# Ten instead of eight weight pairs of the second half's second layer as seven products

## The chip, the cores and the metric

The kernel runs on one core of one Trainium2 chip, with float32 in and out. The time is the device time of the program in microseconds (us); of several executions the median is given. The core has a matrix engine (TensorE, "PE" in the profile, its weight loads "PEld"), VectorE (DVE), ScalarE (ACT), GpSimd (POOL) and SyncE (SP), which here only issues DMAs. Each engine runs its own instructions in the order in which they stand in the program, and an instruction whose data is late holds up everything behind it on that engine.

## The reference

One block on 2048 tokens of width 576: `out = x + attention(layernorm(x)) @ wo + mlp(layernorm(x))`.

```python
xn = layernorm(x)                              # [1, 2048, 576]
q, k, v = heads(xn @ wqkv)                     # 32 heads of 18
idx = pos[:, None] - 2 * arange(8)             # window of 8, dilation 2
attn = softmax(where(idx >= 0, einsum("bhsd,bhswd->bhsw", q, k[idx]) * 18**-0.5, -1e9))
a = einsum("bhsw,bhswd->bhsd", attn, v[idx]).reshape(1, 2048, 576) @ wo
h = einsum("bsd,df->bsf", xn, w1) + b1         # F = 4608
m = einsum("bsf,fd->bsd", h * tanh(softplus(h)), w2)
return x + a + m
```

## The kernel before, in words

**Halves.** The tokens are worked in two halves of 1024 (`hf` 0 and 1). In each half come the projections to query, key and value (`qkv_item`, and `z_part` in the second half), and then the MLP, with the attention of the same half woven in between. At the end `wo_part` multiplies the attention's output by `wo`.

**Numbers in two parts.** Every matrix operand is kept as a rounded high part and a low part, the remainder: a "high" step is a cast on ScalarE, a "low" step a subtraction on VectorE or GpSimd. A product of two such operands takes three matmuls.

**The MLP by pairs.** F is cut into 36 blocks of 128, and two blocks make a pair `q`, 0 to 17. `m1_part` makes the hidden activations of a pair in parts 0 to 5. The second layer of a pair is multiplied one pair later. In the first half, and in the second half from some pair on, that is four chunks of 24 matmuls each (`m2_pair`, line 780; `m2_cols`, line 893). The earlier pairs of the second half go another way: two pairs together (index `e`) are taken as a 2x2 block product by seven products in place of eight (`p_item`, line 872). One such product, an item `k` of 0 to 6 named in `ORD`, is 24 matmuls as a chunk is. `OC` is the number of such twos; with `OC = 4` these are pairs 0 to 7, and pair 8 (`2 * OC`) goes by chunks again, with its activations held as the earlier ones were and split by `a_split`.

**What the seven products need.** Sums of weights T1 to T4: they are made in the first half, where the weights are loaded anyway (`t_sum`, `t_high`, `t_low`, line 301 and on), written to DRAM (`t_keep`) and fetched for their item by `p_fetch`. Sums of activations S1 to S4: `u_sum` (line 814), in place, on VectorE but for two of eight. The high and low part of each left operand: `u_high` (line 820, ScalarE) and `u_low` (line 826, eight of fourteen on GpSimd). Raw activations stand in fixed buffers (`raw_act`). The item's results are added from PSUM into `accP` on VectorE (line 878, and line 876 on ScalarE for the first two); at the end `p_join` joins them.

**The order of the program.** `plan` is a list of steps. A step holds its own functions (`plan[i][0]`: a part of `m1_part`, an item, a chunk) and a list of other work (`plan[i][1]`, filled by `before(i, ...)`), which is issued ahead of them. In the second half an even pair has four items among its steps, an odd pair three:

```python
seq = (0, 1, "N", 2, "N", 3, "N", 4, "N", 5)   # even pair; "N" is an item
for i, p_ in enumerate((0, 1, 2, "N", 3, "N", 4, "N", 5))  # odd pair
```

The number of a step inside its pair is `i` in `spot(hf, q, i)`. An item is issued one `e` after its activations were made: those of pairs 0 and 1 in pairs 2 and 3, and so on.

**Attention.** It is a generator of 73 steps for a half; eight rounds (two units of two heads each) of nine steps: four products of query and key (GpSimd, line 539), one step of softmax, four products with the values (GpSimd, line 577). What VectorE does with a GpSimd product, a reduction (lines 544 and 583), is issued at the next attention step. With the softmax go lines 558 and 560 on VectorE, the exponential on ScalarE (line 564, with a table load before it and another behind it), and then lines 568 to 570. When a round is over, `oT` is transposed on VectorE (line 603). `early` says at which steps of each pair of the second half an attention step is taken; pairs that aren't in it have five.

**Waits between the engines in the second half.** The `out` tag has four PSUM banks, one for each of an item's four results; the next item needs them free again, which the additions of line 878 do. Part 4 of `m1_part` adds into the bank that VectorE reads for the activation of block (1,1) (line 725, the name `rt`), so part 4 waits for that read. These two places, the banks behind `accP` and part 4 behind `rt`, are where TensorE meets VectorE.

## Time and profile before

| | |
|---|---|
| time, median of 3 runs | 1108.59 us (1108.43 to 1108.93) |
| the profiled execution's own time | 1109.51 us |
| its span (first to last instruction) | 1107.7 us |
| granted TensorE clock | 0.999 |
| PE busy | 1100.8 us, 99% |
| VectorE busy | 850.6 us, 77% |
| GpSimd busy | 791.1 us, 71% |
| ScalarE busy | 499.1 us, 45% |
| DMA moved | 271.60 MB, mean 245 GB/s |

Matmuls are pipelined and their ends are modelled, so that a busy PE isn't proof that it runs at its peak; idle time of the other engines costs nothing by itself. Pair q of the first half begins at 24.1 us steps (pair 2 at 139.18, pair 10 at 332.12). In the second half pair 2 begins at 649.46, pair 8 at 786.45, and the last chunks end at 1050 us.

### The profile page before, as it was taken

To read this page: it belongs to the slowest core of one execution; us is meant where nothing else is said; L and a number is where in the kernel's file an instruction comes from. 1 tells how busy PE (TensorE), PEld (TensorE's weight loads), DVE (VectorE), ACT (ScalarE), POOL (GpSimd) and SP (SyncE) were. 2 spreads that over 40 slices of the span, in tenths; PEclk is the share of its full clock that TensorE was granted. 3 is DMA by queue.
4 is the path that set the end of the run, shared out by engine and by line. 5 is a ranking of instruction groups with operands and counts; after the bars stand their busy time and mean duration, and the time that the engine had idled before them with its cause. 6 is when DMAs were issued, how large, how long until landed. Compare 5 with 4: busy or idle time off the path is not lost.

```text
span 1107.7 us, 18208 instructions
## 1 busy us (share of the span) xinstructions
PE 1100.8 (99%) x6550; PEld 1015.3 (92%) x6550; DVE 850.6 (77%) x1367; ACT 499.1 (45%) x917; POOL 791.1 (71%) x639
## 2 busy tenths in 40 slices
PE   9999999999999999999999999999999999999998
PEld 8999899999999999999999888989999999999998
DVE  6368788888889888898656567777876677777786
ACT  5544655544544544545333354434433344343353
POOL 2479777776779688685789667567698976867542
PEclk9999999999999999999999999999999999999999
DMA  6899696868777768676598799656674657776674
GB/s 203 284 311 308 235 343 232 282 239 266 254 259 249 266 222 296 238 263 214 170 323 268 237 358 317 223 192 208 221 222 173 210 195 224 243 288 218 179 234 140
DMA packets 178270, 271.60 MB, mean 245 GB/s; under 512 B 53218, under 2 KB 120068, under 8 KB 178180
## 3 DMA queue, kind: packets, MB, share of 16 engines
q1 hardware_dynamic: 178180, 270.44, 72.0%
q8 instruction: 52, 0.85, 0.3%
q14 instruction: 38, 0.31, 0.1%
HBM read 160.39 MB, written 110.00 MB: 244 GB/s over the span
## 4 chain that ended last, share of the span: by engine, by line
PE 94%; DMA 2%; DVE 2%; ACT 1%; POOL 1%; issue 0%; SPq 0%; DVEq 0%; POOLq 0%
PE h L680 29%; PE po L780 21%; PE po L893 11%; PE pq L348 11%; PE po L872 6%; PE h L686 6%; PE o L1076 5%; PE z L446 4%; DMA t<-kept_t 1%; DMA accP<-in_x 1%; POOL act L732 0%; PE ta L75 0%; DMA acc<-in_x 0%; DVE st L112 0%; DVE u L826 0%
## 5 line engine op out<-in xcount | busy, mean ns | idle before, releaser
L780 PEld LDWEIGHTS po<-w,act 128*128 128x128 f32 x1728 | 236.4, 188 | 6.0 <-POOL act L732 0.4
L780 PE MATMUL po<-w,act 128*128 128x288 f32 x1728 | 240.7, 295 | 0.1
L539 POOL TENSOR_TENSOR pr<-q,kv 128x576 f32<-128x576 f32 x128 | 198.2, 1574 | 9.3 <-DMA q<-q_d 6.1
L732 POOL TENSOR_TENSOR act<-c,act 128x512 fp32r<-128x512 f32 x81 | 107.4, 1326 | 128.1 <-ACT act L731 127.3
L577 POOL TENSOR_TENSOR pv<-L,kv 128x576 f32<-128x576 f32 x128 | 178.1, 1485 | 26.3 <-DVE L L570 21.4
L784 DVE TENSOR_TENSOR acc<-po,acc 128x288 f32<-128x288 f32 x288 | 119.3, 449 | 29.7 <-PE po L780 28.9
L348 PE MATMUL pq<-wq,xt 128*128 128x432 f32 x672 | 136.3, 361 | 0.9 <-ACT xt L81 0.6
L893 PEld LDWEIGHTS po<-w,act 128*128 128x128 f32 x960 | 130.9, 188 | 2.9
L893 PE MATMUL po<-w,act 128*128 128x288 f32 x960 | 132.9, 294 | 0.0
L348 PEld LDWEIGHTS pq<-wq,xt 128*128 128x128 f32 x672 | 125.1, 188 | 7.7 <-ACT xt L81 1.3
L726 ACT ACTIVATE c<-c,b1c 128x512 f32<-128x512 f32 x81 | 58.7, 725 | 138.1 <-DVE c L725 137.8
L680 PE MATMUL h<-xt,t 128*128 128x512 f32 x432 | 110.7, 391 | 0.1
L680 PE MATMUL h<-S,t 128*128 128x512 f32 x432 | 110.5, 391 | 0.0
L583 DVE TENSOR_REDUCE og<-pv 128x144 f32<-128x1152 f32 x64 | 85.9, 1345 | 24.1 <-POOL pv L577 23.9
L680 PE MATMUL h<-xt,wa 128*128 128x512 f32 x432 | 104.1, 390 | 0.0
L714 ACT COPY c<-h 128x512 f32<-128x512 f32 x81 | 47.4, 586 | 124.1 <-PE h L686 73.1
L544 DVE TENSOR_REDUCE L<-pr 128x64 f32<-128x1152 f32 x64 | 85.8, 1342 | 20.9 <-POOL pr L539 20.8
L680 PEld LDWEIGHTS h<-xt,wa 128*128 128x128 f32 x432 | 80.9, 188 | 17.0
L872 PEld LDWEIGHTS po<-pw,u 128*128 128x128 f32 x672 | 92.1, 188 | 3.5 <-DVE accP L878 1.2
L872 PE MATMUL po<-pw,u 128*128 128x288 f32 x672 | 93.8, 295 | 0.8 <-DVE accP L878 0.8
L680 PEld LDWEIGHTS h<-xt,t 128*128 128x128 f32 x432 | 79.1, 188 | 15.1 <-DVE rt L725 0.5
L896 DVE TENSOR_TENSOR accP<-po,accP 128x288 f32<-128x288 f32 x160 | 69.0, 452 | 30.2 <-PE po L893 29.4
(228 smaller groups left out, 1854.3 us busy)
## 6 DMA issues: line engine op xcount, KB each, us to landing
kv<-kv_d SPq DMA_DIRECT2D x64, 396.0 KB, 5.2
kept_t<-t SPq DMA_DIRECT2D x36, 512.0 KB, 4.4
t<-kept_t SPq DMA_DIRECT2D x36, 512.0 KB, 6.5
rw<-in_w SPq DMA_DIRECT2D x36, 320.0 KB, 4.5
kept_wa<-wa SPq DMA_DIRECT2D x18, 640.0 KB, 4.9
kept_w<-w SPq DMA_DIRECT2D x20, 576.0 KB, 4.1
wa<-kept_wa SPq DMA_DIRECT2D x18, 640.0 KB, 5.2
w<-kept_w SPq DMA_DIRECT2D x20, 576.0 KB, 4.3
```

What stands on the lines that cost most here:

```text
L348: nc.tensor.matmul(pq[:, 0:432], XT[:, xi, tok], wt[wi][:, hl, 0:432], start=i == 0, stop=i == len(seq) - 1)
L539: nc.gpsimd.tensor_tensor(out=pr[:, x:x + hh], in0=q[:, j0 + x:j0 + x + hh, None, :].to_broadcast([P, hh, W, CU]), in1=win(kt, 0, CU, j0 + ...
L544: nc.vector.tensor_reduce(L[:, k, j0:j0 + hj].rearrange("p j w h -> p (j w h)"), pr.rearrange("p j w (h d) -> p (j w h) d", h=2), axis=AX, ...
L577: nc.gpsimd.tensor_tensor(out=pr[:, x:x + hj].rearrange("p j d w -> p j w d"), in0=L[:, k, x:x + hj, :, h:h + 1].to_broadcast([P, hj, W, DH]),
L583: nc.vector.tensor_reduce(og[:, c0:c0 + DH, :].rearrange("p d j -> p j d"), pr, axis=AX, op=ALU.add)
L680: nc.tensor.matmul(ph, wt[:, wl, wk * P:(wk + 1) * P], X[:, xs, :], start=first and i == 0, stop=last and i == len(seq) - 1, skip_group_ch ...
L732: nc.gpsimd.tensor_tensor(out=a[:, 1, :], in0=t, in1=a[:, 0, :].bitcast(F32), op=ALU.subtract)
L780: nc.tensor.matmul(po, acts[hf, q, b, j][:, al, tok], done["w2", hf, 2 * q + j][:, wl, c * HC:(c + 1) * HC], start=i == 0, stop=i == 5)
L784: nc.vector.tensor_tensor(out=t, in0=po, in1=t, op=ALU.add)
L872: nc.tensor.matmul(po, units[e, k, qq][:, al, tok], w[:, qq, wl, :], start=i == 0, stop=i == 5)
L893: nc.tensor.matmul(po, acts[hf, q, b, j][:, al, tok], done["w2", hf, 2 * q + j][:, wl, c * HC:(c + 1) * HC], start=i == 0, stop=i == 5)
L896: nc.vector.tensor_tensor(out=t, in0=po, in1=t, op=ALU.add)
```

## The change

`OC` goes from 4 to 5: pairs 8 and 9 of the second half's second layer are taken by seven products as well, and pair 10 takes the part that pair 8 had. With it go these moves:

- In the first half, T1 to T4 are made and written out for pairs 9 and 10 of the weights, too. The similar sums for the projections (`z_load` and on) begin twelve steps later and stand closer together.
- `early` is written anew: odd pairs 3, 5, 7 and 9 have four attention steps (at 0, 2, 4 and 6), even pairs 2 to 8 three (at 0, 4 and 7), and pairs 10 and 11, which had five, have the three that pairs 8 and 9 had. By the end of pair 11 the same number of steps is done as before.
- One sum of activations, S4 of the second pair for item 6 of the first two (`e = 0`, `qq = 1`), is issued behind the step's own instructions instead of ahead of them.
- The preparation of `wo` begins later (from pair 13 instead of 11), and closer together.
- One raw activation of pair `2 * OC` has another buffer than the rotation gives.

```diff
-OC = 4
+OC = 5
...
-                  (0, 1): (("raw", 3), ("mn", 4), ("mn", 1)), (1, 1): (("tt", 0), ("tt", 1))}[b, j][q % {(1, 0): 4, (1, 1): 2}.get((b, j), 3)]
+                  (0, 1): (("raw", 3), ("mn", 4), ("mn", 1)), (1, 1): (("tt", 0), ("tt", 1))}[b, j][3 if (q, b, j) == (2 * OC, 1, 0) else q % {(1, 0): 4, (1, 1): 2}.get((b, j), 3)]
...
-    i = spot(0, 9, 4)
+    i = spot(0, 10, 6)
...
-                d = 30 + 2 * n + (n >= 14) if k else 2 * n if n < 10 else (19, 20, 22, 23, 25, 26, 27)[n - 10]
+                d = 28 * k + (2 * n if n < 10 else (19, 20, 22, 23, 25, 26, 27)[n - 10])
...
-            before(s2, lambda e=e, k=k, qq=qq: u_sum(e, k, qq))
+            plan[s2][0 if (e, k, qq) == (0, 6, 1) else 1].append(lambda e=e, k=k, qq=qq: u_sum(e, k, qq))
...
-    early = {0: (8,), 1: (0, 2, 4, 6, 8), 2: (0, 4, 7), 3: (0, 3, 6), 4: (0, 4, 7), 5: (0, 3, 7), 6: (1, 4, 7),
-             7: (0, 4, 7), 8: (1, 4, 8), 9: (1, 3, 7)}
+    early = {0: (8,), 1: (0, 2, 4, 6, 8), 2: (0, 4, 7), 3: (0, 2, 4, 6), 4: (0, 4, 7), 5: (0, 2, 4, 6), 6: (0, 4, 7),
+             7: (0, 2, 4, 6), 8: (0, 4, 7), 9: (0, 2, 4, 6), 10: (1, 4, 8), 11: (1, 3, 7)}
...
-    i = spot(1, *(11,3))
+    i = spot(1, 13, 0)
...
-        k = i + 10 + (2, 5, 10, 15, 20, 25, 30, 35, 40)[n]
+        k = i + 10 + (2, 5, 8, 12, 15, 19, 23, 27, 31)[n]
```

The change moves instructions on every engine. Three places are shown, in the order of the two programs. In the names `po_0_4_1_0` is PSUM of `e` 0, item 4, second half of its tokens; `u_0_6_1` is the left operand of `e` 0, item 6, second pair; `pr_1_1_0_1` and `pv_1_1_0_1` are attention products of the second half, round 1; `h3_1_3` is a bank of pair 3.

VectorE in pair 3, around item 4 of the first two, before (line 814 is the moved sum, line 878 the additions that free the banks, the last row the read that part 4 waits for):

```order
L725 TENSOR_TENSOR ra0_7255<-h2_1_3_7761,ra0_7255 128x512
L826 TENSOR_TENSOR u_0_5_1_7793<-rm3_7262,u_0_5_1_7793 128x512
L814 TENSOR_TENSOR rm4_7263<-rm4_7263,rm3_7262 128x512
L878 TENSOR_TENSOR accP2_0_7472<-po_0_4_0_0_7811,accP2_0_7472 128x288
L878 TENSOR_TENSOR accP2_0_7472<-po_0_4_0_1_7819,accP2_0_7472 128x288
L878 TENSOR_TENSOR accP2_1_7473<-po_0_4_1_0_7827,accP2_1_7473 128x288
L878 TENSOR_TENSOR accP2_1_7473<-po_0_4_1_1_7835,accP2_1_7473 128x288
L544 TENSOR_REDUCE L_1_1_7745<-pr_1_1_0_0_7747 128x64
L826 TENSOR_TENSOR u_0_6_1_7846<-rm4_7263,u_0_6_1_7846 128x512
L725 TENSOR_TENSOR rt1_7265<-h3_1_3_7777,rt1_7265 128x512
```

The same place now:

```order
L725 TENSOR_TENSOR ra0_7289<-h2_1_3_7795,ra0_7289 128x512
L544 TENSOR_REDUCE L_1_1_7779<-pr_1_1_0_0_7781 128x64
L826 TENSOR_TENSOR u_0_5_1_7827<-rm3_7296,u_0_5_1_7827 128x512
L878 TENSOR_TENSOR accP2_0_7506<-po_0_4_0_0_7845,accP2_0_7506 128x288
L878 TENSOR_TENSOR accP2_0_7506<-po_0_4_0_1_7853,accP2_0_7506 128x288
L878 TENSOR_TENSOR accP2_1_7507<-po_0_4_1_0_7861,accP2_1_7507 128x288
L878 TENSOR_TENSOR accP2_1_7507<-po_0_4_1_1_7869,accP2_1_7507 128x288
L814 TENSOR_TENSOR rm4_7297<-rm4_7297,rm3_7296 128x512
L544 TENSOR_REDUCE L_1_1_7779<-pr_1_1_0_1_7830 128x64
L826 TENSOR_TENSOR u_0_6_1_7880<-rm4_7297,u_0_6_1_7880 128x512
L725 TENSOR_TENSOR rt1_7299<-h3_1_3_7811,rt1_7299 128x512
```

The sum stands behind the four additions; the reduction that stood there has gone ahead of the low step of item 5, and the next one, of `pr_1_1_0_1`, has come to its place.

VectorE in pair 5, the same place of the second two, before:

```order
L826 TENSOR_TENSOR u_1_5_1_8264<-ra_r_7801,u_1_5_1_8264 128x512
L814 TENSOR_TENSOR ra3_7258<-ra3_7258,ra_r_7801 128x512
L583 TENSOR_REDUCE og_1_1_8154<-pv_1_1_0_1_8222 128x8x18
L878 TENSOR_TENSOR accP2_0_7472<-po_1_4_0_0_8280,accP2_0_7472 128x288
L878 TENSOR_TENSOR accP2_0_7472<-po_1_4_0_1_8288,accP2_0_7472 128x288
L878 TENSOR_TENSOR accP2_1_7473<-po_1_4_1_0_8296,accP2_1_7473 128x288
L878 TENSOR_TENSOR accP2_1_7473<-po_1_4_1_1_8304,accP2_1_7473 128x288
L826 TENSOR_TENSOR u_1_6_1_8314<-ra3_7258,u_1_6_1_8314 128x512
L814 TENSOR_TENSOR rm2_7261<-ra1_7256,rm2_7261 128x512
L725 TENSOR_TENSOR rt1_7265<-h3_1_5_8252,rt1_7265 128x512
```

And now:

```order
L583 TENSOR_REDUCE og_1_1_8101<-pv_1_1_1_0_8264 128x8x18
L826 TENSOR_TENSOR u_1_5_1_8302<-ra_r_7841,u_1_5_1_8302 128x512
L814 TENSOR_TENSOR ra3_7292<-ra3_7292,ra_r_7841 128x512
L878 TENSOR_TENSOR accP2_0_7506<-po_1_4_0_0_8318,accP2_0_7506 128x288
L878 TENSOR_TENSOR accP2_0_7506<-po_1_4_0_1_8326,accP2_0_7506 128x288
L878 TENSOR_TENSOR accP2_1_7507<-po_1_4_1_0_8334,accP2_1_7507 128x288
L878 TENSOR_TENSOR accP2_1_7507<-po_1_4_1_1_8342,accP2_1_7507 128x288
L583 TENSOR_REDUCE og_1_1_8101<-pv_1_1_1_1_8305 128x8x18
L603 STREAM_TRANSPOSE oT_1_1_8372<-og_1_1_8101 128x576
L826 TENSOR_TENSOR u_1_6_1_8352<-ra3_7292,u_1_6_1_8352 128x512
L814 TENSOR_TENSOR rm2_7295<-ra1_7290,rm2_7295 128x512
L725 TENSOR_TENSOR rt1_7299<-h3_1_5_8290,rt1_7299 128x512
```

Ahead of the additions one reduction is gone to before the low step; between the additions and the read for part 4 there are a reduction and the transposition more.

ScalarE at the head of pair 4, where the second two begin, before:

```order
L714 COPY ra1_7256<-h1_1_4_7971 128x512
L820 CAST u_1_0_1_7990<-ra_r_7801 128x512
L726 ACTIVATE ra1_7256<-ra1_7256,b1c_122 128x512
L820 CAST u_1_1_1_8006<-rt1_7265 128x512
L820 CAST u_1_2_0_8042<-ra2_7257 128x512
```

And now:

```order
L714 COPY ra1_7290<-h1_1_4_8009 128x512
L564 ACT_TABLE_LOAD
L564 ACTIVATE L_1_1_7779<-L_1_1_7779 128x256
L820 CAST u_1_0_1_8029<-ra_r_7841 128x512
L726 ACT_TABLE_LOAD
L726 ACTIVATE ra1_7290<-ra1_7290,b1c_122 128x512
L820 CAST u_1_1_1_8045<-rt1_7299 128x512
L820 CAST u_1_2_0_8081<-ra2_7291 128x512
```

The exponential of round 1 with its two table loads now stands around the cast that item 0 needs.

More of the change, by code (lines that the diff above doesn't have):

```diff
@@ L1495, in block_kernel @@
     behind_adds.update((at["p", "x", OC - 1, 4], at["p", "x", 0, 4], at["s", 1, 2 * OC, 1]))
-    behind_next.add(at["m", 1, 10, 3])
+    behind_next.add(at["m", 1, 2 * OC + 2, 3])
     T = [0.0]
@@ L1504, in block_kernel @@
             ok[spot(0, q, i)] = i in (0, 3, 7, 9) and (q > 1 or i)
-    marks = [at["q", 0, 2, 0, 1], at["q", 0, 3, 0, 0], spot(0, 1, 0), spot(0, 2 * OC + 1, 0), at["q", 1, 0, 0, 0],
+    marks = [at["q", 0, 2, 0, 1], at["q", 0, 3, 0, 0], spot(0, 1, 0), spot(0, 9, 0), at["q", 1, 0, 0, 0],
              at["z", 0, 0], spot(1, 0, 0)]
```

## The prediction

> **What bounds the kernel now.** The page's busy times come first: TensorE is busy 99% of the span, and the next engine 77%.
>
> ```profile
> span 1107.7 us, 18208 instructions
> PE 1100.8 (99%) x6550; PEld 1015.3 (92%) x6550; DVE 850.6 (77%) x1367; ACT 499.1 (45%) x917; POOL 791.1 (71%) x639
> ```
>
> A busy PE can hide matmuls that are stretched or late, so the chain of work that ended last comes next. In the plain part (chunks of line 893) it is TensorE alone, pair after pair:
>
> ```profile
> 868.62 2.73 PE h L680 x12
> 873.16 3.18 PE po L893 x24
> ...
> 916.88 2.73 PE h L680 x12
> ```
>
> Two pairs take 916.88 - 868.62 = 48.26 us there, and 24 matmuls of the second layer 3.18 us. The busy times by stage show the part with seven products, one row for each of pairs 3, 4 and 5 (the columns: PE, PEld, DVE, ACT, POOL):
>
> ```profile
> 673.84:696.23 22.39, 21.49 (x124) 18.89 (x122) 19.08 (x25) 9.01 (x17) 18.49 (x13) 1.00 0.79 263
> 696.23:720.40 24.17, 24.17 (x147) 22.13 (x146) 18.12 (x34) 11.84 (x18) 13.79 (x11) 1.00 0.64 230
> 720.40:741.37 20.97, 20.97 (x123) 18.95 (x122) 16.06 (x25) 7.93 (x13) 14.31 (x11) 1.00 0.54 187
> ```
>
> Pairs 4 and 5 take 45.14 us together, which is 48.26 less 24 matmuls: TensorE waits for nothing there. Pair 3 takes 22.39 where pair 5, with the same matmuls, takes 20.97: 1.42 us are lost. So a change is worth what it takes from TensorE's instructions, less the waits it makes, and room is scarce in the odd pairs: VectorE is busy for 85% of pair 3 and 77% of pair 5.
>
> **The change part by part.** *The product that goes.* By the order, lines 872 and 893 have 672 and 960 matmuls before, 840 and 768 now: 24 fewer. At 3.18 us for 24 that is -3.2 us; by the two stages above, 45.14 - 48.26 = -3.1, which I take. All of it is on the path, since TensorE is the path.
>
> *The moved sum, pair 3.* VectorE alone, and then TensorE, at that place:
>
> ```profile
> 682.26 1.36 DVE L826 TENSOR_TENSOR u<-rm,u 128x512 fp32r<-128x512 f32 x1 [1.82 <-ACT u L820]
> 683.55 1.77 DVE L814 TENSOR_TENSOR rm<-rm,rm 128x512 f32<-128x512 f32 x1
> 685.24 1.54 DVE L878 TENSOR_TENSOR accP<-po,accP 128x288 f32<-128x288 f32 x4
> 686.70 1.34 DVE L544 TENSOR_REDUCE L<-pr 128x64 f32<-128x1152 f32 x1
> 687.96 0.68 DVE L826 TENSOR_TENSOR u<-rm,u 128x512 fp32r<-128x512 f32 x1
> 688.56 0.68 DVE L725 TENSOR_TENSOR rt<-h,rt 128x512 f32<-128x512 f32 x1
> ```
>
> ```profile
> 684.32 0.61 PE L686 MATMUL h<-xt,wc 128*128 128x512 f32 x2
> 685.74 3.47 PE L872 MATMUL po<-pw,u 128*128 128x288 f32 x24 [0.81 <-DVE accP L878]
> 689.29 1.43 PE L680 MATMUL h<-xt,t 128*128 128x512 f32 x5
> ```
>
> Item 5 (685.74) waits 0.81 us for the additions at 685.24, which stand behind the sum of 1.77. Without it ahead of them the additions start at 683.55, and item 5 at 684.93: that wait is gone. What is late next is part 4 (689.29), which needs the read `rt` of line 725; it could start at 684.93 + 3.18 = 688.1. The reduction that went ahead of the low step at 682.26 costs nothing: VectorE had 1.82 us idle there. Counting from start to start, the path to the read is now: additions 683.55 to 685.01 (1.46), the sum 0.6 to 1.7, a reduction 1.26, a low step 0.60, the read 0.68: 689.2 with the long sum, 688.2 with the short. The reduction moreover waits for GpSimd's `pr_1_1_0_1`:
>
> ```profile
> 676.47 2.82 POOL L539 TENSOR_TENSOR pr<-q,kv 128x576 f32<-128x576 f32 x2
> ```
>
> ```profile
> 684.73 7.04 POOL L539 TENSOR_TENSOR pr<-q,kv 128x576 f32<-128x576 f32 x4
> ```
>
> Such a product has two halves, 2.8 us in the first row and 3.5 in the second. It now starts ahead of GpSimd's own sum, at about 683.0, and ends at 685.9 to 686.6. So part 4 starts at 688.4 to 689.3, or at 690.3 if the low step too is stretched by as much as the sum. Against 689.29: -0.9 to +1.0. I take 0: the sum was long at this very place, and GpSimd is as busy there as before. So 0.81 is won at item 5 and lost again at part 4.
>
> *Four attention steps in an odd pair.* The same place in pair 5:
>
> ```profile
> 727.69 1.77 DVE L814 TENSOR_TENSOR ra<-ra,ra_r 128x512 f32<-128x512 f32 x1
> 729.38 1.34 DVE L583 TENSOR_REDUCE og<-pv 128x144 f32<-128x1152 f32 x1
> 730.65 1.53 DVE L878 TENSOR_TENSOR accP<-po,accP 128x288 f32<-128x288 f32 x4
> 732.11 0.68 DVE L826 TENSOR_TENSOR u<-ra,u 128x512 fp32r<-128x512 f32 x1
> 732.70 0.68 DVE L814 TENSOR_TENSOR rm<-ra,rm 128x512 f32<-128x512 f32 x1
> 733.31 0.68 DVE L725 TENSOR_TENSOR rt<-h,rt 128x512 f32<-128x512 f32 x1
> ```
>
> ```profile
> 734.55 1.55 PE L680 MATMUL h<-xt,t 128*128 128x512 f32 x6
> ```
>
> ```profile
> L603 DVE STREAM_TRANSPOSE oT<-og 128x576 f32<-128x576 f32 x16 | 12.4, 774 | 0.3
> L826 DVE TENSOR_TENSOR u<-rm,u 128x512 fp32r<-128x512 f32 x12 | 12.3, 1023 | 6.2 <-ACT u L820 6.2
> L814 DVE TENSOR_TENSOR rm<-ra,rm 128x512 f32<-128x512 f32 x6 | 6.9, 1152 | 0.9 <-ACT rm L726 0.9
> ```
>
> Now the additions follow the sum at 729.38, to 730.84; then a reduction (1.26), the transposition (0.77), the low step and the next sum (0.60 each), the read (0.68): 734.75 where part 4 starts at 734.55 today. That is +0.2 if nothing is stretched. In this window GpSimd was idle before and now has the fourth step's product; by the group means (1.02 for the low step and 1.15 for the sum, where 0.68 is the least) it is +1.0, and if both are stretched to 1.77, +2.4. I take +0.5. In pair 7 the same path loses the softmax's two instructions and gains one sum, and had no room left: -0.2 to +1.9, taken at +0.1. Pair 9, with lines 568 to 570 in that place, is alike: +0.1.
>
> *The exponential at pair 4.* The cast of item 0's second operand now stands behind it, and the low step behind that:
>
> ```profile
> L560 DVE TENSOR_TENSOR L<-L,m 128x256 f32<-128x256 f32 x16 | 11.7, 731 | 0.5
> ```
>
> ```profile
> L558 DVE TENSOR_REDUCE m<-L 128x32 f32<-128x256 f32 x16 | 6.7, 420 | 0.5
> ```
>
> ```profile
> L820 ACT CAST u<-ra 128x512 fp32r<-128x512 f32 x22 | 13.4, 621 | 9.9 <-DVE ra L814 5.1 <-POOL ra L814 2.6 <-PE po L872 2.1
> ```
>
> ```profile
> L564 ACT ACTIVATE L<-L 128x256 f32<-128x256 f32 x16 | 6.7, 418 | 17.3 <-DVE L L560 17.2
> ```
>
> ```profile
> 698.93 0.69 DVE L826 TENSOR_TENSOR u<-ra_r,u 128x512 fp32r<-128x512 f32 x1 [1.37 <-ACT u L820]
> ```
>
> ```profile
> 700.76 3.33 PE L872 MATMUL po<-pw,u 128*128 128x288 f32 x24
> ```
>
> VectorE's work before that low step ended at 698.93 - 1.37 = 697.56. With lines 558 and 560 (0.42 and 0.73), the exponential (0.42), the cast (0.62) and the low step (0.69) behind one another it is 700.4. The item starts at 700.76 and uses the operand's low part in its sixth matmul, 0.66 later. Cost 0, and 0.5 if the low step too is stretched.
>
> *The first half.* Pairs 9 and 10 get the sums T1 to T4. The fuller of the two before, and one of VectorE's three new instructions:
>
> ```profile
> 332.12:356.20 24.08, 24.08 (x148) 22.09 (x147) 22.16 (x32) 11.32 (x20) 22.09 (x18) 1.00 0.75 250
> ```
>
> ```profile
> L312 DVE TENSOR_TENSOR twT<-twT,twhT 128x576 fp32r<-128x576 f32 x16 | 13.8, 893 | 0.3
> ```
>
> Three of them are 2.7 us, and VectorE loses one of about that kind, the subtraction for the projections that is placed later: 22.16 + 1.8 = 24.0 of 24.08. That is full, yet TensorE's pair shows no loss at 22.2, and what runs over falls into pair 11. I take 0; counted without what goes, 24.9, it runs over by 0.8, the upper bound. The DMAs that go with them (four more writes in each of the two pairs, and later the fetches of seven more items in place of two pairs' weights) stand on SP, behind which no row shown has TensorE waiting. The later `wo` work, the other buffer and the additional splits of pairs 8 and 9 have GpSimd's and VectorE's idle time of pairs 8 to 17 as cover: 0.
>
> *Sum.* -3.1 + 0 + 0.5 + 0.1 + 0.1 = -2.4 us. The profiled execution took 1109.51 us, 0.9 over the median of 1108.59, in equal work; so it would be 1107.1 profiled, and **1106.2** as a median.
>
> **A rule weighed.** In the trace a sum of line 814 takes 0.68 us at 732.70, with GpSimd idle, and 1.77 at 683.55, beside a GpSimd instruction; the additions of line 878, which read PSUM, take the same 1.5 for four in both places. The Trainium skill, "SBUF — State Buffer", section "Who interferes with whom", says that a VectorE instruction with two SBUF inputs and a GpSimd instruction that reads SBUF block each other for the whole instruction, and that reductions never contend. By that rule every low step and sum of the path that meets a GpSimd instruction waits it out, and the time would be that of the slower rival below; by the rows alone it is -2.4. The trace agrees in part: the low step at 687.96 took 0.68 in the middle of GpSimd's products, so that there it was GpSimd that waited.
>
> **The rivals.** *The gain is eaten (no change).* All stretchable instructions of the path take their group means: pair 3 +0.4, pair 5 +1.0, pairs 7 and 9 +0.6 each, 2.6 us in all: -0.5, 1108.1. For it speaks that GpSimd was idle on this path in pairs 5 and 7 and isn't any more; against it, that in pair 5 the additions come 1.3 us earlier, since the reduction went ahead of them.
>
> *The path to part 4 becomes the bound (slower).* Low step and sum are both stretched to 1.77 in each odd pair: +1.0, +2.4, +1.9, +1.9, 7.2 in all, so +4.1, 1112.7. It decides against the change from 1.3 us for each odd pair on, and is slower by over 0.2% from 5.3 in all. Against it: in pair 3, before, one of the two was long and the other was not.
>
> *The first half runs over.* VectorE full in pair 10 delays the freeing of banks by the 0.8 us above, with the forecast's other terms: 1107.0.
>
> **How the numbers follow.** Forecast 0.50, eaten gain 0.28, first half 0.05, slower 0.17. About 0.2%, 2.2 us, is what a measurement of this kernel can tell from no change; the forecast lies just past it, the second and the third within. Faster 0.50, same 0.33, slower 0.17. The range goes from 1104.8 (pair 3 at -0.9, pair 5 at +0.2, pairs 7 and 9 at 0: -3.8; what lies below is left out with some 0.04) up to 1110.8, where slower by over 0.2% begins; most of the slower rival (0.14) is left out.
>
> **What would show it.** In the profile after: 1608 matmuls in lines 872 and 893; pairs 8 and 9 at 45.1 us together; no wait of TensorE on line 878 at item 5 of pair 3; part 4 of pair 5 waiting 0.2 to 1 us on `rt`, that of pairs 7 and 9 hardly. Wrong it would be if a pair of the first half is over 24.2 us, or if the odd pairs take over 22 us: then the waits are the larger term.

## The result, and the profile after

The changed kernel takes 1122.02 us (median of 5, 1119.87 to 1124.9) where the kernel before takes 1108.59. The medians alone give 1.0121 times as long; the ratio on record is 1.0108, with a 95% interval of 1.0082 to 1.0133. The forecast was 1106.2. The profiled execution took 1119.87 us with a span of 1118.1, 10.4 us over the span before. (Beside runs 13, 14 and 17 below, the kernel before itself took 1113.8 to 1116.1 us in half of its executions or more, so the ratios on record there, 0.9960, 1.0005 and 0.9967, mix two levels of that kernel, and these runs' times are set against its 1108.59.)

The page's busy times after:

```profile
span 1118.1 us, 18215 instructions
PE 1101.4 (99%) x6526; PEld 1013.1 (91%) x6526; DVE 861.8 (77%) x1381; ACT 503.2 (45%) x927; POOL 802.7 (72%) x647
```

The 24 matmuls are gone, but TensorE isn't busy for less time, and the span is longer. The waits of TensorE after, without those of the first microseconds (what waits, for what; us in all, how often, the longest). Of these lines the kernel before had none, only one wait of 0.8 us on line 878:

```profile
PE h L680 <- DVE rt L725: 4.3, 3, 1.5
PE h L680 <- DVE c L725: 3.0, 2, 2.3
PE po L872 <- DVE u L826: 1.6, 2, 0.8
PE po L780 <- DVE acc L784: 0.9, 2, 0.8
PE po L893 <- DVE accP L896: 0.7, 1, 0.7
```

Busy times by stage, one row for each pair that lost time: pairs 9, 11 and 15 of the first half, then 3, 5, 7 and, for comparison, 9 of the second (the columns as in the prediction):

```profile
307.51:335.86 28.35, 26.02 (x148) 23.28 (x146) 24.49 (x39) 12.58 (x21) 23.41 (x20) 0.94 0.75 263
359.94:385.12 25.18, 24.41 (x148) 22.03 (x146) 20.44 (x30) 11.65 (x18) 17.27 (x14) 1.00 0.86 316
457.43:483.00 25.57, 24.73 (x147) 22.08 (x146) 19.82 (x31) 12.48 (x22) 21.89 (x23) 1.00 0.68 248
...
680.21:702.90 22.69, 21.20 (x124) 18.94 (x122) 20.57 (x25) 8.91 (x17) 19.54 (x14) 1.00 0.78 260
727.20:751.02 23.82, 21.48 (x124) 18.97 (x122) 20.28 (x28) 7.71 (x13) 17.88 (x13) 1.00 0.62 208
775.19:798.74 23.55, 21.49 (x124) 18.97 (x122) 19.91 (x25) 7.80 (x14) 19.07 (x14) 1.00 0.58 209
822.91:843.81 20.90, 20.90 (x124) 18.91 (x122) 18.64 (x30) 10.91 (x16) 13.83 (x11) 1.00 0.62 214
```

Where the 10.4 us went, by the starts of the pairs before and after:

| place | forecast | before | after | difference |
|---|---|---|---|---|
| first half, pairs 9 and 10 | 0 | 48.23 | 52.43 | +4.2 |
| first half, pair 11 | 0 | 24.15 | 25.18 | +1.0 |
| first half, pair 15 | 0 | 24.17 | 25.57 | +1.4 |
| second half, pairs 3 and 4 | 0 | 46.56 | 46.99 | +0.4 |
| pair 5 | +0.5 | 20.97 | 23.82 | +2.85 |
| pair 7 | +0.1 | 20.90 | 23.55 | +2.65 |
| pairs 8 to 11 (the product) | -3.0 (-3.1 and +0.1) | 106.10 | 103.11 | -3.0 |
| pair 17 to the end | 0 | 94.46 | 95.56 | +1.1 |

The rest, -0.3, lies before pair 0. So the gain came as forecast, and waits that were costed at next to nothing took it back more than four times over. The places are those of one profiled execution: in other profiles of the same first half (runs 2, 5, 7 and 10) pair 9 loses 2.6 or 4.2, pair 10 between 0 and 3.6 and pair 11 between 0 and 2.0 us, 4.7 to 6.2 together. What makes pair 11's share wasn't found.

**Pair 5, after.** GpSimd, VectorE and TensorE on the path to part 4 and item 6 (the last bracket of a row is the idle time before it and what ended it):

```profile
738.48 3.31 POOL L539 TENSOR_TENSOR pr<-q,kv 128x576 f32<-128x576 f32 x2
739.74 0.76 DVE L826 TENSOR_TENSOR u<-ra,u 128x512 fp32r<-128x512 f32 x1
740.42 1.92 DVE L814 TENSOR_TENSOR rm<-ra,rm 128x512 f32<-128x512 f32 x1
742.26 0.68 DVE L725 TENSOR_TENSOR rt<-h,rt 128x512 f32<-128x512 f32 x1
742.99 1.66 PE L680 MATMUL h<-xt,t 128*128 128x512 f32 x6 [1.53 <-DVE rt L725]
744.28 1.28 POOL L826 TENSOR_TENSOR u<-rm,u 128x512 fp32r<-128x512 f32 x1 [2.49 <-ACT u L820]
744.32 1.79 DVE L826 TENSOR_TENSOR u<-rm,u 128x512 fp32r<-128x512 f32 x1
746.17 2.11 PE L872 MATMUL po<-pw,u 128*128 128x288 f32 x14 [0.81 <-DVE u L826]
```

The sum at 740.42 takes 1.92 us beside GpSimd's product, where it took 0.68 before; part 4 waits 1.53. Late from there, item 6's low step (744.32) meets a GpSimd low step, takes 1.79, and item 6 waits 0.81 more in its middle.

**Pair 9 of the first half, after.** GpSimd, ScalarE, VectorE and TensorE around the sums of weights:

```profile
320.39 0.82 POOL L301 TENSOR_TENSOR twT<-rw,twT 128x288 f32<-128x288 f32 x1
321.16 3.34 POOL L577 TENSOR_TENSOR pv<-L,kv 128x576 f32<-128x576 f32 x2
324.32 0.84 POOL L301 TENSOR_TENSOR twT<-rw,twT 128x288 f32<-128x288 f32 x1
325.19 0.67 ACT L307 CAST twhT<-twT 128x576 fp32r<-128x576 f32 x1 [4.17 <-POOL twT L301]
325.89 0.76 DVE L312 TENSOR_TENSOR twT<-twT,twhT 128x576 fp32r<-128x576 f32 x1 [2.59 <-ACT twhT L307]
326.57 0.68 DVE L725 TENSOR_TENSOR c<-h,c 128x512 f32<-128x512 f32 x1
327.31 1.92 PE L680 MATMUL h<-xt,t 128*128 128x512 f32 x4 [2.33 <-DVE c L725]
```

An attention product stands on GpSimd between the second and the third sum of weights. So the third is late, then its cast, then its low part on VectorE, and behind that the read of line 725 that TensorE needs. VectorE had been idle 2.59 us: it wasn't full, it stood behind a late operand. Before, with the same attention steps but no sums of weights in this pair, TensorE had no wait there:

```profile
307.81:331.96 24.15, 24.15 (x147) 22.11 (x146) 21.18 (x34) 10.91 (x19) 19.31 (x17) 1.00 0.74 250
```

**Pair 15 of the first half, after.** The sums of weights for the projections, which the change begins twelve steps later:

```profile
473.63 1.11 POOL L394 TENSOR_TENSOR zB<-zB,zB 128x432 f32<-128x432 f32 x1
474.77 0.61 DVE L402 TENSOR_TENSOR zB<-zB,zhT 128x432 fp32r<-128x432 f32 x1 [3.50 <-POOL zB L394]
475.29 0.68 DVE L725 TENSOR_TENSOR c<-h,c 128x512 f32<-128x512 f32 x1
476.03 1.66 PE L680 MATMUL h<-xt,t 128*128 128x512 f32 x6 [0.67 <-DVE c L725]
```

It is the same chain once more. GpSimd makes the sum T4 (line 394) late; the low step of T2 (line 402) writes over what T4 reads and stands behind it, and behind that stands the read that TensorE needs.

### The profile page after: what moved, and what is told of

Read it like the earlier page. It is cut to its first block, busy times and chain, and to the rows that moved or that the text cites. A ratio compares the mean times of both kernels' runs of the same rounds, so it can differ in the third digit from the quotient of the medians.

```text
span 1118.1 us, 18215 instructions
## 1 busy us (share of the span) xinstructions
PE 1101.4 (99%) x6526; PEld 1013.1 (91%) x6526; DVE 861.8 (77%) x1381; ACT 503.2 (45%) x927; POOL 802.7 (72%) x647
## 4 chain that ended last, share of the span: by engine, by line
PE 77%; POOL 10%; issue 5%; DVE 5%; DMA 2%; ACT 1%; SPq 0%; POOLq 0%; DVEq 0%
PE h L680 23%; PE po L780 16%; PE pq L348 11%; PE po L893 7%; PE po L872 6%; PE o L1076 5%; PE h L686 4%; PE z L446 4%; POOL pv L577 2%; POOL pr L539 2%; POOL act L732 2%; DVE u L826 1%; POOL u L826 1%; POOL tt L240 1%; DMA accP<-in_x 1%
## 5 line engine op out<-in xcount | busy, mean ns | idle before, releaser
L780 PEld LDWEIGHTS po<-w,act 128*128 128x128 f32 x1728 | 236.6, 188 | 7.6 <-DVE acc L784 1.8
L780 PE MATMUL po<-w,act 128*128 128x288 f32 x1728 | 241.0, 295 | 1.1 <-DVE acc L784 0.9
L577 POOL TENSOR_TENSOR pv<-L,kv 128x576 f32<-128x576 f32 x128 | 181.7, 1511 | 23.7 <-DVE L L570 13.7
L732 POOL TENSOR_TENSOR act<-c,act 128x512 fp32r<-128x512 f32 x75 | 99.7, 1329 | 121.2 <-ACT act L731 118.6
L872 PEld LDWEIGHTS po<-pw,u 128*128 128x128 f32 x840 | 115.3, 188 | 5.3 <-DVE u L826 2.2
L872 PE MATMUL po<-pw,u 128*128 128x288 f32 x840 | 117.8, 295 | 1.6 <-DVE u L826 1.6
L726 ACT ACTIVATE c<-c,b1c 128x512 f32<-128x512 f32 x75 | 54.4, 725 | 133.2 <-DVE c L725 133.0
L893 PEld LDWEIGHTS po<-w,act 128*128 128x128 f32 x768 | 104.6, 188 | 3.3 <-DVE accP L896 1.2
L893 PE MATMUL po<-w,act 128*128 128x288 f32 x768 | 106.3, 295 | 0.7 <-DVE accP L896 0.7
L680 PEld LDWEIGHTS h<-S,t 128*128 128x128 f32 x432 | 77.9, 188 | 13.2 <-ACT rm L714 0.5
L714 ACT COPY c<-h 128x512 f32<-128x512 f32 x75 | 43.9, 585 | 96.8 <-PE h L686 52.8
```

The costliest lines, as they stand in the source:

```text
L577: nc.gpsimd.tensor_tensor(out=pr[:, x:x + hj].rearrange("p j d w -> p j w d"), in0=L[:, k, x:x + hj, :, h:h + 1].to_broadcast([P, hj, W, DH]),
L680: nc.tensor.matmul(ph, wt[:, wl, wk * P:(wk + 1) * P], X[:, xs, :], start=first and i == 0, stop=last and i == len(seq) - 1, skip_group_ch ...
L732: nc.gpsimd.tensor_tensor(out=a[:, 1, :], in0=t, in1=a[:, 0, :].bitcast(F32), op=ALU.subtract)
L780: nc.tensor.matmul(po, acts[hf, q, b, j][:, al, tok], done["w2", hf, 2 * q + j][:, wl, c * HC:(c + 1) * HC], start=i == 0, stop=i == 5)
L872: nc.tensor.matmul(po, units[e, k, qq][:, al, tok], w[:, qq, wl, :], start=i == 0, stop=i == 5)
L893: nc.tensor.matmul(po, acts[hf, q, b, j][:, al, tok], done["w2", hf, 2 * q + j][:, wl, c * HC:(c + 1) * HC], start=i == 0, stop=i == 5)
```

## The experiments

**One part each: attention in the first half (1), three steps (2), four steps in the kernel before (3), the moved sums of the projections in the kernel before (4).**

```diff
 # 1, on the changed kernel
-spot(0, 1, 0), spot(0, 9, 0)
+spot(0, 1, 0), spot(0, 2 * OC + 1, 0)
-rate = (1.15, 0.4, 0.5, 0.8, 1.15, 1.25, 0)
+rate = (1.15, 0.4, 0.5, 0.886, 1.15, 1.25, 0)
 # 2, on the changed kernel (behind_next is emptied with it)
-3: (0, 2, 4, 6), 5: (0, 2, 4, 6), 7: (0, 2, 4, 6), 9: (0, 2, 4, 6)
+3: (0, 3, 6), 5: (0, 3, 7), 6: (1, 4, 7), 7: (0, 4, 7), 9: (0, 4, 7), 12 to 15: (0, 2, 4, 5, 7, 9)
 # 3, on the kernel before
-3: (0, 3, 6), 5: (0, 3, 7), 7: (0, 4, 7)
+3, 5, 7: (0, 2, 4, 6), 10: (1, 4, 8), 11: (1, 3, 6, 9)
 # 4, on the kernel before: the two edits to the chain of z_load and on
```

Expected of 1: 

> The changed kernel, but in the first half attention runs at its slower rate (0.5) up to pair 10, as far as sums of weights are made, and at 0.886 in place of 0.8 behind it, so that as many steps fit. If pair 9 was lost because GpSimd had attention steps at the faster rate and the sums T1 to T4 in one pair, pair 9 goes back from 28.35 to 24.15 us, 4.2 us less in all (about 1117.8 for 1122.0). If the sums alone are too much for the pair, whatever the attention does, pair 9 stays above 27 us. Pairs 11 and 15, which get a little more attention, keep their 1.0 and 1.4 us or lose up to 1 us more.

Expected of 2: 

> The changed kernel with three attention steps in place of four in pairs 3, 5, 7 and 9 of the second half (where they stood before), and six in place of five in pairs 12 to 15, where no seven-product items are left. If the fourth step makes the waits, pairs 5 and 7 go back from 23.82 and 23.55 us to 20.9 to 21.3, so that 5.0 to 5.7 us go (about 1116.5); the sixth step in the later pairs may take up to 2 of them back. If the waits come from the tenth pair's other traffic (more fetches, the moved sum, the splits), pairs 5 and 7 stay above 23 us.

Expected of 3: 

> The kernel before with nothing changed but four attention steps in pairs 3, 5 and 7 of the second half at steps 0, 2, 4 and 6, three in pair 10 and four in pair 11. If the fourth step alone makes the waits, pair 5 takes 23.8 and pair 7 23.5 us, and pair 3 about as much as before or up to 1 us more: 5.5 to 6.5 us slower than before (1114 to 1115). If it needs something else of the change beside it, pairs 5 and 7 stay under 21.5 us and the time within 1 us of 1108.6.

Expected of 4: 

> The kernel before with nothing changed but the place of the projections' weight sums: twelve steps later and closer together. If the move alone makes the waits of pairs 11 and 15 of the first half, those take 25.2 and 25.6 us and the time is 2.4 us over before (about 1111.0). If these waits come from what the sums T1 to T4 of pairs 9 and 10 push ahead of them, pairs 11 and 15 stay at 24.15 us and the time at 1108.6.

Measured: 1 takes 1119.87 us (1116.78 to 1124.34), pair 9 24.69 for 28.35; but pair 13 takes 25.12, pair 15 25.25 and the stretch from pair 17 0.7 more. 2 takes 1122.44: pairs 3, 5 and 7 take 21.51, 20.90 and 21.49 for 22.69, 23.82 and 23.55, and pairs 12 to 14 with the sixth step lose 2.9, 0.7 and 3.7. 3 takes 1116.0, ratio 1.0063 (1.0046 to 1.0079). Its pairs 5 and 7, and TensorE's wait in pair 8 for a fetch of a sum of weights, which no theory had:

```profile
721.00:744.82 23.82, 21.47 (x124) 18.97 (x123) 20.09 (x27) 7.73 (x13) 17.97 (x13) 1.00 0.63 209
...
768.99:790.93 21.94, 21.28 (x123) 19.02 (x122) 18.23 (x25) 7.92 (x14) 18.71 (x14) 1.00 0.55 182
...
PE po L872 <- DMA pw<-kept_T: 1.2, 1, 1.2
```

4 takes 1110.04, ratio 1.0015 (1.0004 to 1.0025): pair 15 takes 25.61, while pairs 9 to 11 are unhurt.

```profile
355.82:379.97 24.15, 24.15 (x147) 22.11 (x146) 22.22 (x33) 12.45 (x19) 17.53 (x14) 1.00 0.71 253
...
452.29:477.90 25.61, 24.71 (x148) 22.07 (x146) 19.81 (x31) 12.51 (x22) 21.92 (x23) 1.00 0.67 248
```

What follows: the fourth step alone makes the whole loss of pair 5 (2.85 in run 3), and of pair 7's 2.65 us it makes 1.05; with three steps (run 2) pair 5 loses nothing and pair 7 still 0.6. The moved sums by themselves make the loss of pair 15, and not that of pair 11. The loss of pair 9 needs both the sums of weights and the faster attention: in 4 it has the faster attention without the sums and loses nothing, in 1 the sums with the slower attention and loses 0.5.

**A GpSimd product left out (5, 10), wo (6), the sum put back (7).**

```diff
 # 5 and 10, on the changed kernel; 5 with (1, 5, 6), (1, 7, 6), 10 with (1, 5, 4), (1, 7, 4)
-nc.gpsimd.tensor_tensor(out=pr[...], in0=..., in1=..., op=ALU.mult)
+nc.gpsimd.memset(pr[...], 0.0)      # in the steps at these spots
 # 6, on the kernel before
-i = spot(1, *(11,3))
+i = spot(1, 13, 0)
-(2, 5, 10, 15, 20, 25, 30, 35, 40)
+(2, 5, 8, 12, 15, 19, 23, 27, 31)
 # 7, on the changed kernel
-plan[s2][0 if (e, k, qq) == (0, 6, 1) else 1].append(lambda ...)
+before(s2, lambda ...)
```

Expected of 5: 

> The changed kernel; of the fourth attention step of pair 5 and of pair 7 of the second half (step 6) the product is left out: GpSimd fills its tile with zeros instead, which reads nothing. Every other engine has the same instructions in the same order. If part 4 is late because VectorE's two-input instructions stand still while GpSimd multiplies, the sum of line 814 in pair 5 takes 0.68 us for 1.92 and the low step of line 826 in pair 7 takes 0.68 for 1.75; part 4 then waits 0.2 to 0.4 us for 1.53 and 1.26, item 6's wait is 0 to 0.3, and pairs 5 and 7 take 21.1 to 21.7 and 21.3 to 22.4 us for 23.82 and 23.55. If it is the longer queue on VectorE (a reduction and a transposition more), these durations do not matter and both pairs stay above 23.3 us.

Expected of 10: 

> The changed kernel; of pairs 5 and 7 of the second half the product of the attention step at place 4 is left out, and GpSimd fills its tile with zeros: this is the product that GpSimd runs beside the path to part 4 (the one at place 6 runs behind it, as the run before showed). If VectorE's two-input instructions stand still while GpSimd multiplies, the sum of line 814 in pair 5 takes 0.68 us for 1.92 and the low step of line 826 in pair 7 takes 0.68 for 1.75; part 4 waits 0.2 to 0.5 us for 1.53 and 1.26, and the pairs take 21.1 to 22.3 us for 23.82 and 23.55. If the long durations have another reason, or GpSimd's instruction only moves up and another one takes its place beside the path, both pairs stay above 23.3 us.

Expected of 6: 

> The kernel before with nothing changed but the preparation of wo: from pair 13 in place of 11 and closer together. If that makes the wait in the last chunks, the stretch from pair 17 on is 1.0 us longer (1109.7 for 1108.7) and the wait is behind line 896 again; if that wait comes from when the last attention steps fall, the time is that of before.

Expected of 7: 

> The changed kernel with the moved sum put back ahead of the step. If moving it only shifts the wait from item 5 to part 4 of pair 3, as forecast, pair 3 takes 22.3 to 23.2 us for 22.69 and the time stays within 0.5 us of the changed kernel. If the move is worth the whole wait with four attention steps, pair 3 gets 0.8 us longer or more; in the kernel before with four steps it took 23.15.

Measured: 5 takes 1120.96 and its pairs 5 and 7 23.81 and 23.54; the step chosen was the wrong one, since GpSimd is a step behind the order, and what it multiplies beside the path is the product of place 4. In 10 that is the one left out; the same place of pair 5:

```profile
739.74 1.09 POOL L539 MEMSET pr<- 128x576 f32 x2
740.99 0.69 DVE L826 TENSOR_TENSOR u<-ra,u 128x512 fp32r<-128x512 f32 x1
741.60 0.68 DVE L814 TENSOR_TENSOR rm<-ra,rm 128x512 f32<-128x512 f32 x1
742.21 0.68 DVE L725 TENSOR_TENSOR rt<-h,rt 128x512 f32<-128x512 f32 x1
742.94 1.66 PE L680 MATMUL h<-xt,t 128*128 128x512 f32 x6 [0.23 <-DVE rt L725]
744.24 1.85 POOL L826 TENSOR_TENSOR u<-rm,u 128x512 fp32r<-128x512 f32 x1 [3.41 <-ACT u L820]
744.26 0.68 DVE L826 TENSOR_TENSOR u<-rm,u 128x512 fp32r<-128x512 f32 x1
```

VectorE has the same instructions in the same order as after, and the same reduction and transposition ahead of them. The sum takes 0.68 for 1.92, part 4 waits 0.23 for 1.53, item 6 not at all; in pair 7 the low step takes 0.69 for 1.75; and the pairs take 21.43 and 21.39. So of the 5.5 us lost in the two pairs 4.55 go with that product, beside which VectorE stood still, and the longer queue costs the other 0.95. In the last two rows it is GpSimd whose low step takes 1.85 for 1.28: the two block each other, and either may lose: after, VectorE lost at 744.32. By the Trainium skill, "SBUF — State Buffer", section "Who interferes with whom", this is what a VectorE instruction with two SBUF inputs and a GpSimd instruction that reads SBUF do, while one that only writes doesn't block; the first half agrees with these rows. No row here shows the second: the fill with zeros (739.74 and 1.09 long) was over before the low step began at 740.99.

6 takes 1109.35, ratio 1.0007 (0.9998 to 1.0016), which isn't told from no change; its trace has the wait of the last chunks, and its stretch from pair 17 to the end is 95.44 us for 94.46:

```profile
PE po L893 <- DVE accP L896: 0.7, 1, 0.7
```

7 takes 1120.12, within the spread of the changed kernel, with pair 3 at 23.01, where the profiles with the moved sum and four steps have 22.69 (the changed kernel), 23.03 (run 1), 23.00 (5), 22.93 (10) and 22.82 (9): with four steps the move shifts the wait, as forecast, and is worth nothing that shows.

**What is left of the change without the waits (8, 9, 11, 12; in the expectations 8, 11 and 12 are the first, second and third repair).** The second half with three steps in pairs 3, 5 and 7 and four in 4, 6 and 8; several first halves.

```diff
 # 8: early as below; rate 0.5, in pairs 4 and 8 0.65, 0.8 from pair 10; the sum T4 of the projections two steps earlier
+3: (0, 3, 6), 4: (0, 2, 4, 7), 5: (0, 3, 7), 6: (0, 2, 4, 7), 7: (0, 4, 7), 8: (0, 2, 4, 7), 9: (0, 2, 4, 6)
 # 9: the first half alone
+ok[spot(0, q, i)] = i in ((0, 7, 9) if q <= 2 * OC else (0, 3, 7, 9)) and (q > 1 or i)
 # 11: 9, with early as in 8 but 6 and 8: (0, 2, 5, 7); low part of T2 one step later; wo from spot(1, 12, 0)
 # 12: 9, with early as in 8 but 6 and 8: (0, 3, 5, 8); that chain two steps later; wo from spot(1, 12, 3)
```

Expected of 8: 

> The changed kernel with the waits taken out one by one: three attention steps in pairs 3, 5 and 7 and four in pairs 4, 6 and 8 (steps 0, 2, 4 and 7), pair 9 as it is; in the first half the faster rate from pair 10 on, pair 9 at 0.5 and pairs 4 and 8 at 0.65; and the chain's sum T4 two steps earlier, ahead of the small GpSimd instructions of pair 15. If the causes are those named, pairs 9, 11 and 15 of the first half are at 24.1 to 24.3 us, pairs 3, 5 and 7 of the second at 20.9 to 21.6 and pairs 4, 6 and 8 at 24.2: 3.0 us for the product, 0.5 to 1.0 for pair 3, less 1.0 at the end, so 1105.5 to 1107 for 1108.7 of before. If attention simply no longer fits, the fourth step in the even pairs costs 1 us or more each and the time is 1110 or over.

Expected of 9: 

> The changed kernel; only in the first half no attention step is taken at step 3 of a pair that makes sums of weights (pairs 1 to 10), where it puts its GpSimd product between these sums. Pairs 9 and 10 keep three steps each (0, 7, 9) and pair 11 gets one more. If that one place, and not the number of steps, makes the wait of pair 9, pairs 9 and 10 take 24.1 to 24.3 us for 28.35 and 24.08 (26.78 and 26.15 in another run of the same first half), and the time is 4 to 5 us under the changed kernel's (1117 to 1118). If three steps beside the sums are too many wherever they stand, pair 9 or 10 stays over 25 us.

Expected of 11: 

> The changed kernel, second repair: no attention at step 3 beside the sums of weights; three attention steps in pairs 3, 5 and 7 and four in pair 4 (0, 2, 4, 7), 6 and 8 (0, 2, 5, 7); in the chain of the projections' sums the low part of T2 one step later, behind the read that part 4 waits for in pair 15; wo prepared from pair 12. If each cause is the one named, pairs 9, 10, 11 and 15 take 24.1 to 24.3 us, pairs 3, 5 and 7 of the second half 20.9 to 22.4, pairs 6 and 8 24.2, and the wait in the last chunks is gone: 1105.5 to 1106.5. Each repair that fails costs its 0.7 to 1.5 us again, and with two of them failed the kernel is no faster than before.

Expected of 12: 

> As the second repair, with other choices where several are open: pairs 6 and 8 take their four steps at 0, 3, 5 and 8, the chain of the projections' sums starts two steps later with its own order kept, and wo is prepared from step 3 of pair 12. The same pairs are expected at the same times; where it differs from the second repair, the place of that one step is what decides. If the wait of pair 15 comes from the small GpSimd instructions of the layer norm there, two steps may move it by 0 to 1.4 us either way.

Measured: 8 takes 1113.17; pairs 5 and 7 are at 20.98 and 20.89 as before, but pairs 6 and 8 lose 1.0 and 0.7, pairs 4 and 10 of the first half 1.2 and 1.8, and pair 15 is at 25.57: moving T4 two steps ahead on GpSimd changed nothing. 9 takes 1121.45: pair 9 is at 24.62, but pair 10 at 25.13 and pair 11 at 28.61. In 11 (1116.65) and 12 (1117.0) pairs 4 to 9 of the second half have no wait at all; 11 loses 4.4 in pair 13, where wo is now prepared; in 12 pair 13 loses nothing, pair 16 loses 0.2, and the end is 94.9. In the first half pairs 9 and 10 lose in both as in 9, and pair 11 4.5 in 11 and 1.7 in 12; pairs 15 and 16 lose 0.45 and 1.1 in 11, and 3.6 and 2.4 in 12.

**The first half by hand (13 to 18, the fourth to the ninth repair).** All have the second half of 11 (the expectation of 13 names the third repair, which has other places in pairs 6 and 8), wo from step 3 of pair 12, and the second chain's T4 on VectorE. The steps of the first half in pairs 5 to 10, and where the one step too many stands:

```diff
 # 13: 5: (3, 7), 6: (3, 7), 7: (3, 7, 9), 8: (3, 7, 9), 9: (7, 9), 10: (7, 9)
 # 14: 5: (3, 7, 9), 6: (3, 7), 7: (3, 7, 9), 8: (3, 7), 9: (7, 9), 10: (7, 9)
 # 15: 5, 6, 7: (3, 7), 8: (3, 7, 9), 9: (7, 9), 10: (7, 9), and 11: (0, 3, 7, 9)
 # 16: as 15, but 11 as before, and 17: (3, 7)
 # 17: as 15, but 11 as before, and 10: (5, 7, 9)
 # 18: as 15, but 11 as before, and one step more in pair 0
```

Expected of 13: 

> The changed kernel with the second half of the third repair (pairs 6 and 8 at 0, 2, 5, 7; wo prepared from step 3 of pair 12), which left no wait in pairs 4 to 9 and at the end, and a first half with the same number of attention steps by the end of pair 10, moved by hand: 5 to 8 take 2, 2, 3 and 3 steps, 9 and 10 two each. The sum T4 of the second chain (line 394) is on VectorE in place of GpSimd. If GpSimd's attention beside the sums of weights is what costs, pairs 9, 10 and 11 are at 24.1 to 24.6 us and pairs 5 to 8 too, since only pair 4 lost time with a step at 3 in the first repair; if the wait of pair 15 is the one behind GpSimd's late T4, that pair goes from 25.57 to 24.2 to 24.7. Then the sum is 3.0 us won, 0 to 1.5 lost: 1105.5 to 1107.5. If every place in the first half is full, the loss comes up again in one of pairs 5 to 8 or 16 with 1 to 3 us, and the time is 1108 to 1110.

Expected of 14: 

> The fourth repair with one attention step of the first half moved from pair 8 to pair 5 (5: 3, 7, 9; 8: 3, 7), so that no step at place 3 beside the sums of weights is the one in which GpSimd's first product with the values waits for lines 568 to 570 on VectorE (in pair 8 of the fourth repair it did, and the third sum of weights behind it made the wait of 1.24 us). If that step's wait is the cause, pair 8 goes from 25.65 to 24.1 us and the time to 1106.5 to 1107.0. If three steps with one at place 3 are too many in any pair with sums of weights, pair 5 takes 25 us or more, and the time stays at 1108.

Expected of 15: 

> The fourth repair with the steps of pairs 5 to 10 of the first half at (3, 7), (3, 7), (3, 7), (3, 7, 9), (7, 9), (7, 9), and a fourth step at place 0 of pair 11, which makes no sums of weights. The theory from the runs so far: a step at place 3 costs time beside the sums only where GpSimd comes into the pair already late, because the pair before ended with a step at 9 or this one has one at 0 (pairs 6 and 8 of the fifth repair, 8 of the fourth, 4 and 10 of the first, 9 of the changed kernel); then pairs 6 to 10 all take 24.1, pair 5 about 24.3, and pair 11 24.1 or, if the chain of projections' sums is late there as in the run without place 3, up to 2.7 more: 1106.5 to 1107, or up to 1109.5. If the number of steps decides, a pair of 5 to 8 takes 25 us or more.

Expected of 16: 

> The same, but with the one step in pair 17 instead of 11, so that every step from pair 11 to 17 comes one place later in its round. Pairs 5 to 10 are as in the sixth repair by either theory. Pair 11 is at 24.15; the small instructions of the layer norm, which go with one step of round 4, come one step later in pair 15, so that its 0.45 us may go or grow to 1.5: 1106.0 to 1108.0.

Expected of 17: 

> The sixth repair, but the one step that pair 11 could not take goes to place 5 of pair 10, behind the last of the three sums of weights (issued at steps 2, 3 and 4), and pair 11 has its three steps as in the fourth repair. By the theory that only a GpSimd product ahead of a sum of weights makes VectorE late, pairs 5 to 11 take 24.1 to 24.4 us and all the rest is as in the fourth repair less the 1.57 us of its pair 8: 1106.4 to 1107.0. If three steps in pair 10 are too many wherever they stand, pair 10 or 11 takes 25 us or more and the time is 1108 or over.

Expected of 18: 

> The sixth repair, but its surplus step goes ahead of pair 1, into the stretch of pair 0 where GpSimd is busy for 4.3 of 7 us, so that pairs 1 to 10 have 21 steps in all, each pair at the places of the sixth repair, each step one later in its round than there, and pairs 11 to 17 have exactly the steps of the fourth repair. If the number of steps and their places decide, and not which step of the round it is, pairs 1 to 11 take 24.1 to 24.4 us, pair 15 24.6, all else as in the fourth repair: 1106.4 to 1107.0. If it matters which step it is, one of pairs 0 to 10 takes 0.5 to 4 us more, and the time is 1107 to 1111.

| run | time (us) | lost in the first half |
|---|---|---|
| 13 | 1108.19 (1107.96 to 1108.67) | pair 8 1.57, 15 0.45, 5 0.2 |
| 14 | 1112.60 (1111.48 to 1116.24) | pair 6 2.3, 8 4.2, 15 0.45, 5 0.2 |
| 15 | 1114.68 (1110.42 to 1117.86) | pair 11 4.4, 15 0.5, 5 0.1 |
| 16 | 1109.60 (1107.55 to 1113.79) | pair 12 0.5, 17 1.2, 5 0.2, 11 0.1 |
| 17 | 1108.55 (1107.43 to 1109.26) | pair 10 1.5, 15 0.4, 5 0.2 |
| 18 | 1109.60 (1109.08 to 1110.42) | pair 5 1.4, 0 0.7, 4 and 6 0.6 each, 15 0.4, less 0.4 in 1 |

With T4 on VectorE, pair 15 goes from 25.6 to 24.6, and so it does in 11, where the low step of T2 comes later: the wait stood behind GpSimd's late T4, as the rows of pair 15 have it. The last table is a string of half misses: the theory of 14, that only the step whose product waits for the softmax costs time, fell with its pairs 6 and 8. That of 15 and 16, a step at place 3 that GpSimd comes to late, is borne out by their pairs 6 to 10, which lose nothing with 21 steps in pairs 1 to 10; but 17, whose surplus step stands behind the sums, loses 1.5 in pair 10 all the same. No place was found for the 22nd step that costs less than about 1.4 us (16: 1.2 in pair 17, 0.5 in 12 and 0.1 in 11, with 0.45 less in 15). The lowest median, that of 13, is within 0.1% of the kernel before; its waits:

```profile
PE warm L65 <- POOL ident masks.py:199: 1.3, 1, 1.3
PE ta L75 <- ACT xn L180: 1.3, 2, 0.8
PE h L680 <- DVE c L725: 1.2, 1, 1.2
...
PE h L680 <- DVE rt L725: 0.3, 1, 0.3
```

Its span is 1106.2 us, 1.5 under the span before: 3.0 from the product and 0.9 from pair 3, less 2.2 in the first half and 0.3 at the end, which leaves 0.1 for the rest. The 0.9 can't be put down to the change, since pair 3 of the kernel before varies as much by itself (next section); without it some 0.6 us of gain are left.

## Why the prediction was wrong

- *The product that goes*, -3.1: right. Pairs 8 to 11 are 3.0 shorter, with no wait in pairs 8 and 9.
- *The moved sum*, 0 with -0.9 to +1.0: right in kind; that the size came out is in part luck. Item 5's wait is gone, part 4 waits in its place, +0.3 in this profile. The 0.81 us of before turned out to vary from profile to profile: the pair takes 22.39 before, and 21.60 and 21.42 in runs 4 and 6, whose pair has the same instructions. In run 4 TensorE came to it 1.1 us later and VectorE, which waits there for GpSimd's line 858 and that for a DMA of x, only 0.3 later, so that most of the wait was covered. Against 21.60 and 21.42 the changed kernel's 22.69 is a loss of 1.1 to 1.3. It goes with the fourth step and not with the moved sum: with three steps and the moved sum (runs 2, 8 and 11 to 18) this pair takes 21.2 to 22.4.
- *Four steps in an odd pair*, +0.5 and +0.1: this step failed, in one term. The queue was counted rightly: with the durations of 0.68 it gave +0.2 at part 4 of pair 5, and run 10, where they are 0.68, measures a wait of 0.23 on the matmuls (0.47 on their weight loads, and the pair is 0.46 longer). The durations were wrong. The prediction took 0.68 for each sum and low step but for a small allowance, with GpSimd's product known to lie beside them; they took 1.92 in pair 5, and in pair 7 the low step 1.75. The rule of the Trainium skill that the prediction weighed, and set aside on one counterexample (the 0.68 at 687.96), gave the slower rival: +2.4 and +1.9 for these two pairs, where +2.85 and +2.65 were measured. That it came so near is in part luck. It took two instructions as stretched where one was, so that part 4 waited only 1.53 and 1.26; and it had no term for a second wait, that of item 6 in its middle (0.81 and 0.80).
- *Pair 9*, +0.1: 20.90, no loss. The slower rival would have had +1.9 here, so it too was not right everywhere.
- *The exponential at pair 4*, 0 with 0.5: +0.1.
- *The first half*, 0 with at most +0.8: this step failed outright. It added up VectorE's busy time, which came out just full, and asked nothing of the order on GpSimd. But the wait comes through GpSimd, whose sums stand behind attention, and by way of ScalarE to a VectorE that was idle 2.59 us. The rate of 0.8 in pairs 9 and 10 was harmless as long as no sums were made there (run 4). Nor was it asked where the moved sums of the projections come to stand: 1.4 us in pair 15.
- *wo*, 0: +1.0 at the end, by its place alone (the end in run 6's profile; its time isn't told from no change, and its pair 3 was 1.0 shorter). That wo stands in the last chunks beside the last softmax is in the trace; which of its instructions makes the wait wasn't isolated.

The conditions that the prediction named for being wrong (a pair of the first half over 24.2 us, odd pairs over 22) are the two that came. What stays open is why pairs 1 to 10 of the first half bear 21 steps in the places of 15 and 16 and no 22nd, what makes the loss of pair 11, and why the loss moves by 1 to 2 us with small shifts of the order.

## What to carry to other kernels

A term of "0, hidden by idle time" is only as good as the order on the engine that feeds the hidden work: before adding work to a full stretch, list what stands ahead of each new instruction on its own engine, and on the engine of its operand. Where two engines block each other, price a path twice, with the free and with the blocked duration, and look which instruction of the other engine is running at that microsecond; that choice was worth 4.5 us here, more than the gain. And a schedule without waits is a tuned state: a change that takes 3 us of matmuls out and moves five lists of places has to be re-tuned in each list before it shows its gain; here the re-tuned lists left 0.4 us of the 3 in the median (1108.19 for 1108.59).

## What the runs showed of the hardware

The wait of 2.33 us in pair 9 cost 4.2 because TensorE's granted clock fell behind it; in run 2 the same wait cost 2.6. Here are the 3.6 us behind the wait in the changed kernel, and in run 2, which has the same first half and the same wait of 2.33 us in that place:

```profile
327.40:331.00 3.60, 3.60 (x10) 2.82 (x11) 3.57 (x9) 1.75 (x3) 2.26 (x2) 0.53 1.02 337
```

```profile
327.60:331.20 3.60, 3.60 (x21) 3.26 (x22) 3.57 (x9) 1.80 (x3) 2.21 (x2) 1.00 1.01 334
```

The clock is 0.53 in one and 1.00 in the other, 10 matmuls against 21. That is a stretch of about 3.4 us at half clock, which costs some 1.7 us of work (an estimate from the two rows). Over the profiled executions the clock fell behind 12 of the 19 waits of 1.78 us and more (not behind 2.33 in run 2, nor behind 2.15 in run 12), and behind none of the 31 from 1.0 to 1.74; two rows of run 10 stand close together:

```profile
353.60 2.76 PE L680 MATMUL h<-xt,t 128*128 128x512 f32 x6 [1.78 <-DVE c L725]
...
697.25 1.66 PE L680 MATMUL h<-xt,t 128*128 128x512 f32 x6 [1.74 <-DVE rt L725]
```

So a wait of some 2 us may cost 2 or 4. It may be a part of why the changed kernel spreads over 5 us from execution to execution. In run 1 the two executions with a mean clock of 1.000 took 1116.78 and 1117.02 us, those with 0.998 and 0.997 took 1122.73 and 1124.34; but a stretch of half clock takes only 0.0015 off the mean and 1.7 us, so something else differs too, and only one execution of each run was profiled. The Trainium skill, "TensorE: Matmul & The Clock Gate", Part 1, says that the clock is halved after at least one idle window of about 3.4 us, and that this window runs freely; by that it would depend on where in the window a wait falls. The dependence on chance and the length of the slow stretch agree with these rows; that 1.8 us of waiting is enough is less than the page says.
